# A half step for the value matmuls in an attention scheduler, and its rules in a table by stretch

## The chip, the cores and the metric

The kernel runs on one core of one Trainium2 chip. The metric is device time in microseconds (us), the median of several runs. One further execution was recorded by the hardware profiler, and all views of the profile are of that one. Engines: PE does matmuls (PEld is its weight load), ACT evaluates functions such as exp, DVE and POOL do elementwise work, SP issues most DMAs.

## The reference

Four layers follow each other, each added to a residual stream `x` of 2048 tokens by 512 features, each with 32 heads of 16 features and with a layer norm ahead:

```python
x = x + A(ln(x)); x = x + B(ln(x)); x = x + A(ln(x)); x = x + B(ln(x))

def A(x):                       # full softmax attention
    q, k, v = heads(x @ wqkv)
    p = softmax(einsum("bhqd,bhkd->bhqk", q, k) * Dh ** -0.5)
    return merge(einsum("bhqk,bhkd->bhqd", p, v)) @ wo

def B(x):                       # linear attention with a learned feature map
    q, k, v = heads(x @ wqkv)
    phi = lambda t: concat(softmax(t @ w_phi), softmax(-(t @ w_phi)))
    kv, z = einsum("bhsf,bhsd->bhfd", phi(k), v), phi(k).sum(over s)
    return merge(phi(q) @ kv / (phi(q) . z + 1e-6)) @ wo
```

Both A layers share their weights, and so do both B layers. The change is in A alone.

## The kernel before

`LayerA.attention` emits one A layer, `self.li` being 0 for the first and 1 for the second. The heads are taken in 8 sets of four (`g`), the queries in 4 blocks of 512 (`j`); a pair of these is a group `G`, 32 in all. A group goes over 16 tiles of 128 keys (`kt`). For each key tile there are two *halves* in the sense of heads (`h` is 0 or 1), so a layer has 32 × 16 × 2 = 1024 score tiles of 128 by 1024.

The work of one score tile: `score_cols` (line 1266) issues eight small matmuls side by side on PE, with 32 keys and 512 queries each, into a pair of PSUM banks (`psS`, two such pairs). ACT then takes exp of the whole tile (line 1273) into one of six SBUF buffers `p`. When both tiles of a key tile are there, `pvs` (line 1316) multiplies them with the values: eight fp32 matmuls with 64 keys by 32 value columns as weights and 512 queries as the moving side, summed over the 16 key tiles in a pair of accumulator banks. There are two such pairs, `double` and `pm`; one holds the running group, the other is for everything else.

Some score tiles don't go to ACT. `power_task` lets DVE compute the exponential, with some sixteen instructions per tile (lines 1284 to 1304), into the one buffer `px`. Its scores go into a free pair of accumulator banks, are issued eight key tiles ahead (`LEAD`), and only for groups 1 to 25 (`POWERS`). In the text such a tile is a tile of powers.

Beside these, PE has side work, in two streams of Python generators: the projections of the next octet of heads (`octet`: values, then from a given step on keys and queries, then norms, whose maximum at line 1028 ends the octet), the output projection of finished blocks, and in the first layer the preparation of weights. Side work takes the free pair of banks (`take`) and goes in units of eight matmuls. After the norms come, an event of the scheduler emits the key and query loads of the next two sets of heads (`load_rows` and `load_shift`, lines 1245 to 1253) on SP's queue; the value loads (line 988) are on the same queue.

The order of all this is written out by hand: a planner in Python runs a model of the engines while it emits the instructions. `pe` is the model's time on PE, `act` that on ACT. A score tile counts `UNIT` (0.217 us), a value step `STEP` (0.864), an exp `EXP` (0.904). In each turn of the loop a score tile goes first, as soon as its bank pair is free (`free`). Otherwise the planner asks what fits before the next score tile must start if ACT is not to wait (`due`): first a value step if one is ready, then a tile of powers, then a unit of side work. A value step may end up to `LATE` = 0.2 us after that time. A tile of powers may be issued while side work is pending only from step `EAGER[self.li]` on, 100 in the first attention layer and 0 in the second; `self.now` is the step, that is 16 G + kt, so a layer has 512.

Of the kernel before, what the change touches and what calls it, by code (L numbers as in the profile page):

```python
# [24 lines left out]
NT = S // P  # L25
# [25 lines left out]
FAR = 1e9  # L51
UNIT = 0.217
STEP = 0.864
EXP = 0.904
THERE = 0.54
BACK = 1.11
# [5 lines left out]
POWERS = 26  # L62
LEAD = 8
RING = 4
EAGER = (100, 0)
VBUSY = 0.4
LATE = 0.2
SIDE = 0.0
ALIGN = 0.05
BACKGROUND = 100  # L70
# [7 lines left out]
def mha_hedgehog_stack(ctx, tc, x_in, a_wqkv, a_wo, b_wqkv, b_wphi, b_wo, out, shmin=SHMIN):  # L78
    nc = tc.nc
# [798 lines left out]
    class LayerA:  # L878
# [426 lines left out]
            self.pt[(G, kt, half)] = pt  # L1305
            self.done[(G, kt, half)] = self.plan.end + 0.15

        def pvs(self, G, kt, acc):
            g, j = self.groups[G]
            o, par = g // 2, g % 2  # L1310
            for hh in range(4):
                pt = self.pt[(G, kt, hh // 2)]
                x = kt * 132 + hh * 33 + 17 * par
                for h in range(2):
                    r = slice(64 * h, 64 * h + 64)
                    nc.tensor.matmul(acc[h][32 * hh:32 * hh + 32, :], self.oct[o]["v"][r, x:x + 32],  # L1316
                                     pt[r, hh % 2, :], start=(kt == 0), stop=(kt == NT - 1), skip_group_check=True)

        def load_ob(self, j):
            if j == 0:  # L1320
# [126 lines left out]
        def attention(self, extra, nxt):  # L1447
# [8 lines left out]
            plan = self.plan  # L1456
# [20 lines left out]
            tiles = deque((G, kt, h) for G in range(len(self.groups)) for kt in range(NT) for h in range(2))  # L1477
            pvq = deque((G, kt) for G in range(len(self.groups)) for kt in range(NT))
            estart, slots, acc, pvdone = [], [0.0] * 6, {}, 0
            pe = act = 0.0  # L1480
            self.yts, self.sp = [0.0] * RING, 15.0
            power, pxfree = set(), 0.0
            lost = 0.0
            with tc.manual_schedule(engines=COMPUTE):
                while pvq or any(s.gens for s in self.streams):
                    plan.now = pe
                    plan.advance(pe)
                    for e in list(events):
                        if self.now >= e[0] and e[1]():
                            events.remove(e)  # L1490
                            e[2]()
                    if tiles:
                        free = estart[-2] + BACK if len(estart) > 1 else 0.0
                        due = act - THERE
                        if not slots:
                            free = due = FAR
                        if free <= pe:
                            G, kt, h = tiles.popleft()
                            if (G, kt, h) in power:
                                continue  # L1500
                            self.now = kt + NT * G
                            assert self.groups[G][0] in self.kq
                            self.scores(G, kt, h)
                            slots.sort()
                            start = max(act, pe + THERE, slots.pop(0))
                            lost += start - act
                            act = start + EXP
                            estart.append(start)
                            self.done[(G, kt, h)] = start + BACK
                            pe += UNIT  # L1510
                            continue
                    else:
                        free = due = FAR
                    need = self.side_need()
                    ready = 0
                    for G, kt in pvq:
                        if any(self.done.get((G, kt, h), FAR) > pe for h in range(2)):
                            break
                        ready += 1
                    first = need is not None and need[1][0] == "pe" and len(need[1]) > 2 and ready <= 1  # L1520
                    for turn in range(2):
                        if first == (turn == 0):
                            if need is not None:
                                s, (kind, *what) = need
                                if kind == "M":
                                    soon = pvq and (NT - pvq[0][1] <= ALIGN * what[0] or pvq[0][0] not in acc)
                                    if min(self.pfree) <= pe and not soon:
                                        s.need, s.holds = None, True
                                        break
                                elif pe + what[0] <= (free + SIDE if len(what) == 1 else max(due, free)):  # L1530
                                    plan.now = pe + what[0]
                                    s.need = None
                                    pe += what[0]
                                    self.stream_need(s)
                                    break
                        elif ready:
                            G, kt = pvq[0]
                            if (G in acc or min(self.pfree) <= pe) and pe + STEP <= max(due, free) + LATE:
                                if G not in acc:
                                    acc[G] = self.take()  # L1540
                                pvq.popleft()
                                idx, banks2 = acc[G]
                                self.pvs(G, kt, banks2)
                                if kt == NT - 1:
                                    pvdone = G + 1
                                    self.spawn(self.norm_task(G, idx, banks2), STEP + 0.3)
                                pe += STEP
                                plan.now = pe
                                for h in range(2):
                                    if (G, kt, h) in power:  # L1550
                                        pxfree = pe + 0.3
                                    else:
                                        slots.append(pe + 0.35)
                                    del self.pt[(G, kt, h)]
                                break
                        if turn == 0 and tiles and pxfree <= pe and (need is None or self.now >= EAGER[self.li]) and plan.clock["V"] <= pe + VBUSY:
                            n = NT * tiles[0][0] + tiles[0][1] + LEAD
                            G, kt = n // NT, n % NT
                            if 0 < G < POWERS and self.groups[G][0] in self.kq and plan.now >= self.landed[self.groups[G][0]] and pvq[0][0] in acc and \
                               NT - pvq[0][1] >= 3 and min(self.pfree) <= pe and pe + UNIT <= max(due, free):  # L1560
                                power.add((G, kt, 1))
                                pxfree = FAR
                                idx, ps = self.take()
                                self.score_cols(*self.groups[G], kt, 1, ps)
                                pe += UNIT
                                plan.now = pe
                                self.spawn(self.power_task(G, kt, 1, idx, ps))
                                break
                    else:
                        pe = min(max(free, pe), pe + 0.02) if free > pe else pe + 0.02  # L1570
                        assert pe < 2000.0
                plan.now = FAR / 2
                plan.advance(FAR)
# [707 lines left out]
```

## Time and profile before

| | us |
|---|---|
| runs | 2494.02, 2494.33, 2494.68, median 2494.33 |
| the profiled execution | 2493.94 |
| its span, first to last instruction | 2492.2 |
| first attention layer, first to last exp (71.0 to 1009.2) | 938.2 |
| second attention layer (1311.7 to 2239.7) | 928.0 |
| ACT busy in exp, first and second attention layer | 929.62 (1004 exps), 923.06 (997 exps) |
| mean granted clock of PE | 0.989 |

A row of the matmul order or of the chain begins with the start in us and the length in us. A row of a busy-time view begins with a stretch, from and to, then its length, then busy time and, in parentheses, the number of instructions; behind these stand the granted clock, the share of the DMA engines' time and GB/s. Of the 2048 score tiles of both layers 2001 go to ACT, so 47 are tiles of powers.

### The profile page before, as it was taken

To read this page: it belongs to the slowest core of one execution; us is meant where nothing else is said; L and a number is where in the kernel's file an instruction comes from. 1 tells how busy PE (TensorE), PEld (TensorE's weight loads), DVE (VectorE), ACT (ScalarE), POOL (GpSimd) and SP (SyncE) were. 2 spreads that over 40 slices of the span, in tenths; PEclk is the share of its full clock that TensorE was granted. 3 is DMA by queue.
4 is the path that set the end of the run, shared out by engine and by line. 5 is a ranking of instruction groups with operands and counts; after the bars stand their busy time and mean duration, and the time that the engine had idled before them with its cause. 6 is when DMAs were issued, how large, how long until landed. Compare 5 with 4: busy or idle time off the path is not lost.

```text
span 2492.2 us, 103433 instructions
## 1 busy us (share of the span) xinstructions
PE 2303.5 (92%) x46698; PEld 1083.9 (43%) x46698; DVE 1602.2 (64%) x2866; ACT 2136.6 (86%) x2379; POOL 530.6 (21%) x644
## 2 busy tenths in 40 slices
PE   6999999999989999899889999999999999998998
PEld 4444444444434443445344444444443444444543
DVE  8233456756667455889973666667567652469897
ACT  6899999999999999444539999999999999993553
POOL 3111111121110000356441112111111000005553
PEclk9999999999999999999899999999999999999999
DMA  5412240132045331100124004203300441120003
GB/s 195 69 27 44 49 82 20 43 48 50 3 104 126 118 112 62 52 35 18 61 72 77 19 7 63 34 3 51 65 4 15 88 128 48 66 70 26 26 1 112
DMA packets 114925, 142.86 MB, mean 57 GB/s; under 512 B 64184, under 2 KB 69928, under 8 KB 112168
## 3 DMA queue, kind: packets, MB, share of 16 engines
q1 hardware_dynamic: 113288, 133.38, 21.7%
q8 instruction: 367, 6.01, 1.0%
q0 software_dynamic: 1184, 2.77, 0.3%
q14 instruction: 86, 0.70, 0.1%
HBM read 62.16 MB, written 41.94 MB: 42 GB/s over the span
## 4 chain that ended last, share of the span: by engine, by line
ACT 58%; PE 14%; issue 12%; DVE 12%; POOL 2%; DMA 0%; ACTq 0%; POOLq 0%; SPq 0%; DVEq 0%
ACT p L1273 57%; PE double L1316 3%; PE s L1266 2%; DVE su L1691 1%; PE pbv L1618 1%; PE pk L1618 1%; PE pq L1618 1%; PE pm L713 1%; DVE yt L1908 1%; DVE f L1683 1%; POOL f L1700 1%; DVE f L1684 1%; PE fl L1950 1%; DVE mx L1680 1%; PE pm L1316 1%
## 5 line engine op out<-in xcount | busy, mean ns | idle before, releaser
L1273 ACT ACTIVATE p<-s 128x1024 f32<-128x1024 f32 x2001 | 1853.0, 1063 | 19.2 <-PE s L1266 15.2
L1266 PE MATMUL s<-kq 49*32 49x512 f16 x15136 | 789.7, 381 | 102.7 <-ACT p L1273 86.8
L1266 PEld LDWEIGHTS <-kq 49*32 49x32 f16 x15872 | 385.8, 89 | 881.8 <-issue 795.9
L1316 PE MATMUL double<-p,v 64*32 64x512 f32 x9064 | 612.7, 591 | 0.0
L1316 PE MATMUL pm<-p,v 64*32 64x512 f32 x6944 | 475.6, 589 | 0.0
L977 POOL TENSOR_TENSOR yt<-yt,yt 128x512 f32<-128x512 f32 x64 | 84.8, 1324 | 764.1 <-DVE yt L974 742.3
L1316 PEld LDWEIGHTS double<-p,v 64*32 64x32 f32 x9064 | 174.1, 106 | 30.9 <-issue 6.2
L1618 PEld LDWEIGHTS <-xnTa 128*128 128x128 f16 x1152 | 111.1, 99 | 155.1 <-DVE f L1684 26.4
L1350 DVE SCALAR_TENSOR_TENSOR xt<-pm,c_oA,xt 128x512 f32<-128x512 f32 x102 | 76.2, 747 | 155.9 <-PE pm L713 151.9
L1097 POOL TENSOR_TENSOR sq<-stg 128x512 bf16<-128x512 f16 x48 | 57.7, 1202 | 478.1 <-DVE stg L1005 250.6
L1316 PEld LDWEIGHTS pm<-p,v 64*32 64x32 f32 x6944 | 135.0, 106 | 21.6 <-issue 2.6
L1700 POOL TENSOR_TENSOR f<-f,su 128x1024 f32<-128x1024 f32 x58 | 112.2, 1934 | 116.3 <-DVE su L1694 103.4
L974 DVE STREAM_TRANSPOSE yt<-double 128x512 f32<-128x512 f32 x72 | 47.3, 695 | 112.3 <-PE double L1316 112.1
L1618 PE MATMUL pbv<-wbv,xnTa 128*128 128x512 f16 x384 | 93.9, 397 | 21.7 <-DVE f L1684 21.7
L1685 ACT ACTIVATE f<-f,c_pB 128x1024 f32<-128x1024 f32 x62 | 70.4, 1148 | 49.6 <-DVE f L1684 42.3
L1706 ACT ACTIVATE fk<-f 128x1024 f16<-128x1024 f32 x30 | 31.7, 1057 | 74.7 <-POOL f L1700 74.7
L713 PEld LDWEIGHTS <-wA 64*32 64x32 f16 x4608 | 75.9, 93 | 44.8 <-issue 9.2
L974 DVE STREAM_TRANSPOSE yt<-pm 128x512 f32<-128x512 f32 x56 | 36.8, 696 | 90.4 <-PE pm L1316 90.1
L1000 DVE TENSOR_SCALAR tq<-double,c_qk 128x512 f32<-128x512 f32 x28 | 21.0, 749 | 108.0 <-PE double L713 101.0
L1618 PE MATMUL pq<-wbqk,xnTa 128*128 128x512 f16 x384 | 88.4, 379 | 0.7 <-DVE vt L1645 0.7
L1618 PE MATMUL pk<-wbqk,xnTa 128*128 128x512 f16 x384 | 88.1, 379 | 0.0
L1950 PE MATMUL fl<-wbo,obB 128*128 128x512 f16 x312 | 76.7, 403 | 8.7 <-ACT raw L1902 3.6
(342 smaller groups left out, 3083.2 us busy)
## 6 DMA issues: line engine op xcount, KB each, us to landing
kq<-stg SPq DMA_DIRECT2D x168, 128.0 KB
xd<-xt SPq DMA_DIRECT2D x40, 512.0 KB
xt<-xd SPq DMA_DIRECT2D x40, 512.0 KB
v<-vyt SPq DMA_DIRECT2D x384, 16.0 KB
oD<-osp SPq DMA_DIRECT2D x24, 256.0 KB
ob<-oD SPq DMA_DIRECT2D x8, 768.0 KB
xt<-in_A_x_dram SPq DMA_DIRECT2D x8, 512.0 KB
wbqk<-dBqk SPq DMA_DIRECT2D x2, 2048.0 KB
```

The costliest lines, as they stand in the source:

```text
L713: nc.tensor.matmul(ps[h][c, :], w[r, c], x[r], start=(n == 0), stop=(n == of - 1), skip_group_check=True)
L974: nc.vector.transpose(ys[u].rearrange("p a b -> p (a b)"), ps[u])
L977: nc.gpsimd.tensor_tensor(ys[0], ys[0], ys[1], ALU.add)
L1097: nc.gpsimd.tensor_tensor(sq, hi, hi, ALU.mult)
L1266: nc.tensor.matmul(banks2[u][32 * c:32 * c + 32, :], self.side(g, half, 64 * u, 0, kt * P + 32 * c, 32), self.side(g, half, 64 * u, 1, j * ...
L1273: nc.scalar.activation(pt, s, AF.Exp, scale=EXPS)
L1316: nc.tensor.matmul(acc[h][32 * hh:32 * hh + 32, :], self.oct[o]["v"][r, x:x + 32], pt[r, hh % 2, :], start=(kt == 0), stop=(kt == NT - 1), ...
L1350: nc.vector.scalar_tensor_tensor(xt[:, u, :], ps[h], con["oA"], xt[:, u, :], op0=ALU.mult, op1=ALU.add)
L1618: nc.tensor.matmul(dst, xnT[:, a, c, t * P:(t + 1) * P], w(b, c), start=(i == 0 and c == 0), stop=(i == 2 and c == NC4 - 1))
L1685: nc.scalar.activation(f, f, AF.Exp, scale=con["pB"])
L1700: nc.gpsimd.tensor_tensor(f3, f3, self.part_sums(f3, slice(0, 64), factor), ALU.mult)
L1950: nc.tensor.matmul(ps2[:, u, :], obs[j][:, c, a, t * P:(t + 1) * P], wo[:, b, c, :], start=(c == 0 and i == 0), stop=(c == NC4 - 1 and i = ...
```

## The change

A value step can be parted. `pvs` takes a slice of the 512 queries; a parted step issues its eight matmuls once for queries 0 to 255 and, in a later turn, once more for queries 256 to 511. The model counts `HALF` = 0.434 us for each. Between the two, score tiles and side work may be issued, but no other value step. The first half goes out only where the whole doesn't fit, and never for key tile 0 of a group.

The two constants `LATE` and `EAGER` give way to a table `RULES` with a row per attention layer and an entry per stretch of 32 steps. An entry has three numbers. The first says when a tile of powers may be issued: 2 always, 1 only with no side work pending, 0 never. The second is the lateness allowed to a whole step or a second half, the third that allowed to a first half. The first layer has entries of its own for each stretch; the second has (2, 0.02, 0.0) throughout.

```diff
+HALF = 0.434
-EAGER = (100, 0)
-LATE = 0.2
+RULES = (((2, 0.2, 0.05), (2, 0.2, 0.05), (2, 0.05, 0.01), (2, 0.1, 0.01), (2, 0.02, 0.2), (2, 0.02, 0.1), (2, 0.05, 0.0), (2, 0.02, 0.1),
+          (2, 0.05, 0.1), (2, 0.2, 0.0), (2, 0.02, 0.05), (2, 0.1, 0.1), (2, 0.02, 0.2), (0, 0.02, 0.02), (2, 0.02, 0.01), (1, 0.02, 0.02)),
+         ((2, 0.02, 0.0),) * 16)
...
-        def pvs(self, G, kt, acc):
+        def pvs(self, G, kt, acc, part=slice(0, 512)):
...
-                    nc.tensor.matmul(acc[h][32 * hh:32 * hh + 32, :], self.oct[o]["v"][r, x:x + 32],
-                                     pt[r, hh % 2, :], start=(kt == 0), stop=(kt == NT - 1), skip_group_check=True)
+                    nc.tensor.matmul(acc[h][32 * hh:32 * hh + 32, part], self.oct[o]["v"][r, x:x + 32],
+                                     pt[r, hh % 2, part], start=(kt == 0), stop=(kt == NT - 1), skip_group_check=True)
...
+                    eager = RULES[self.li][self.now // 32][0]
...
-                            if (G in acc or min(self.pfree) <= pe) and pe + STEP <= max(due, free) + LATE:
+                            room = max(due, free) - pe
+                            late, short = RULES[self.li][self.now // 32][1:]
+                            if half is not None and HALF <= room + late:
+                                pvq.popleft()
+                                idx, banks2 = acc[G]
+                                self.pvs(G, kt, banks2, slice(256, 512))
+                                half, step = None, HALF
+                            elif half is None and (G in acc or min(self.pfree) <= pe) and (STEP <= room + late or kt and HALF <= room + short):
                                 if G not in acc:
                                     acc[G] = self.take()
+                                idx, banks2 = acc[G]
+                                if STEP > room + late:
+                                    self.pvs(G, kt, banks2, slice(0, 256))
+                                    half = kt
+                                    pe += HALF
+                                    plan.now = pe
+                                    break
                                 pvq.popleft()
-                                idx, banks2 = acc[G]
                                 self.pvs(G, kt, banks2)
+                                step = STEP
+                            else:
+                                step = None
+                            if step:
...
-                        if turn == 0 and tiles and pxfree <= pe and (need is None or self.now >= EAGER[self.li]) and plan.clock["V"] <= pe + VBUSY:
+                        if turn == 0 and tiles and pxfree <= pe and (eager == 2 or eager and need is None) and plan.clock["V"] <= pe + VBUSY:
```

More of the change, by code (lines that the diff above doesn't have):

```diff
@@ L1481, in attention @@
             self.yts, self.sp = [0.0] * RING, 15.0
-            power, pxfree = set(), 0.0
+            power, pxfree, half = set(), 0.0, None
             lost = 0.0
@@ L1537, in attention @@
                             G, kt = pvq[0]
-                            if (G in acc or min(self.pfree) <= pe) and pe + STEP <= max(due, free) + LATE:
+                            room = max(due, free) - pe
[6 more added lines that the diff above has]
+                            elif half is None and (G in acc or min(self.pfree) <= pe) and (STEP <= room + late or kt and HALF <= room + short):
                                 if G not in acc:
                                     acc[G] = self.take()
+                                idx, banks2 = acc[G]
[5 more added lines that the diff above has]
+                                    break
                                 pvq.popleft()
-                                idx, banks2 = acc[G]
                                 self.pvs(G, kt, banks2)
+                                step = STEP
+                            else:
+                                step = None
+                            if step:
                                 if kt == NT - 1:
                                     pvdone = G + 1
-                                    self.spawn(self.norm_task(G, idx, banks2), STEP + 0.3)
-                                pe += STEP
+                                    self.spawn(self.norm_task(G, idx, banks2), step + 0.3)
+                                pe += step
                                 plan.now = pe
```

## The prediction

> **What bounds the kernel now.** I read the page first, then busy time by stage, then the chain of waits in two stretches of 40 us, then the order of the matmuls around one irregular place of that chain.
>
> ```profile
> PE 2303.5 (92%) x46698; PEld 1083.9 (43%) x46698; DVE 1602.2 (64%) x2866; ACT 2136.6 (86%) x2379; POOL 530.6 (21%) x644
> ACT 58%; PE 14%; issue 12%; DVE 12%; POOL 2%; DMA 0%; ACTq 0%; POOLq 0%; SPq 0%; DVEq 0%
> L1273 ACT ACTIVATE p<-s 128x1024 f32<-128x1024 f32 x2001 | 1853.0, 1063 | 19.2 <-PE s L1266 15.2
> ```
> ```profile
> 71.00:543.20 472.20, 466.36 (x503) 1.00 0.24 45
> 71.00:1009.20 938.20, 929.62 (x1004) 1.00 0.27 64
> 1311.70:2239.70 928.00, 923.06 (x997) 1.00 0.23 49
> ```
> The second fence is ACT's busy time in exp (line 1273) by stretch: from, to, length, busy, count. The two attention stages last 938.2 and 928.0 us, 1866 of the span's 2492, and ACT is busy in 99% of both. PE's 92% on the page looks like a rival bound, but the chain runs 58% over ACT. So each attention stage takes as many exps as it holds, times the interval from one exp to the next, and the change can act through these two numbers alone.
>
> The interval is where the time hides. ACT's records (1063 ns) are longer than the interval and overlap, so an exp may start late without any idle time: the 15.2 us of waiting for scores says little. The starts in the chain of waits say more:
>
> ```profile
> 603.24 0.71 ACT p L1273
> 603.94 0.20 issue
> 604.14 0.88 ACT p L1273
> 605.02 0.04 issue
> 605.07 1.63 ACT p L1273 x2
> 606.69 0.37 issue
> 607.07 0.70 ACT p L1273
> ...
> 622.58 1.63 ACT p L1273 x2
> ...
> 633.68 1.63 ACT p L1273 x2
> ```
> ```profile
> 1607.85 1.63 ACT p L1273 x2
> ...
> 1625.36 1.63 ACT p L1273 x2
> ...
> 1636.46 1.63 ACT p L1273 x2
> ```
> From 603.24 to 604.14 is 0.90, the shortest interval; two exps take 1.83 (603.24 to 605.07). The two merged into "x2" take 2.00 (605.07 to 607.07): 0.17 too much. What PE did there:
>
> ```profile
> 604.53 0.41 PE L1266 MATMUL s<-kq 49*32 49x512 f16 x8
> 604.75 1.05 PE L1316 MATMUL pm<-p,v 64*32 64x512 f32 x16
> 605.61 0.41 PE L1266 MATMUL s<-kq 49*32 49x512 f16 x8
> 605.82 0.41 PE L1266 MATMUL double<-kq 49*32 49x512 f16 x8
> 606.20 0.41 PE L1266 MATMUL s<-kq 49*32 49x512 f16 x8
> 606.41 1.05 PE L1316 MATMUL pm<-p,v 64*32 64x512 f32 x16
> 607.27 0.41 PE L1266 MATMUL s<-kq 49*32 49x512 f16 x8
> ```
> A score tile holds PE for 0.22 (604.53 to 604.75), a value step for 0.86 (604.75 to 605.61), together 1.08 against the 0.90 that ACT needs for one exp. The score buffers forgive one such step in two exps. When a second step follows behind the next score (here one had preceded 604.53), the score after it is 0.17 late, and ACT with it. The planner lets that happen: LATE is 0.2, and 0.17 is less.
>
> **The change part by part.** *(1) Tighter lateness, with halves as the way out.* In the second attention stage a whole step may now end only 0.02 late, a half not at all; in the first stage the table keeps 0.2 for wholes in stretches 0, 1 and 9 and gives 0.1 to 0.02 elsewhere. After a whole step has used up the slack, the room behind the next score is 0.90 − 0.22 = 0.68: a whole (0.86) is refused, a half (0.43) fits and leaves 0.25. So the 0.17 should go. How often does it occur? Three "x2" in each of the two stretches of 40 us above, 0.075 per us; over 938 and 928 us that is 70 and 70, an estimate, worth 12.0 and 11.8 us. Three of the first stage's 16 stretches keep their rule, which leaves 13/16 × 12.0 = 9.7, together 21.5. I take three quarters, 16: some halves of the first stage may still be late by up to 0.2, and a queue of value steps that drains more slowly can stall something else. Bounds: 0 and 21.5; beside that, halves in the place of wholes can save the 0.01 or 0.02 that a single whole step costs (I count nothing, at most 6 over both stages).
>
> *(2) What a split costs PE.* A whole step has 16 matmul records and 16 weight loads, a split one 32 and 32. No half step is in the trace. The nearest rows: 16 matmuls of 512 fp16 columns, two units of side work, on the same 64x32 tiles, and the 16 loads of a whole value step:
>
> ```profile
> 1319.06 0.61 PE L713 MATMUL pm<-xnTb,wAv 64*32 64x512 f16 x16
> 1319.49 0.40 PE L1266 MATMUL s<-kq 49*32 49x512 f16 x8
> ```
> ```profile
> 604.53 0.36 PEld L1316 LDWEIGHTS pm<-p,v 64*32 64x32 f32 x16
> ```
> Sixteen pairs of load and matmul pass in 0.43 (1319.06 to 1319.49), which is half of 0.86. And 16 fp32 loads take 0.36, less than 0.43, so they can lie under the matmuls. I cost the split at nothing; what covers a small excess is the 0.25 left behind a half. The other bound: if no load were hidden, a half would take 0.43 + 0.36, that is 0.36 too long, 0.11 more than the cover; 13/16 × 70 + 70 = 127 split steps have 254 halves, 28 us. A gain is excluded, since the columns are the same. I take 0, because the fp16 row has the same count of loads and matmuls on the same tiles.
>
> The Trainium skill speaks against this: its page "TensorEngine Tiling (Array Packing)", section "Instruction Overhead", gives each matmul some 60 cycles of overhead on this chip and warns against splitting a small dimension. At the 2.4 GHz of "TensorE: Matmul & The Clock Gate" (its opening table) that would be 25 ns, an estimate, 0.4 us for the 16 extra matmuls one behind another, and 127 × (0.4 − 0.25) = 19 us of loss by it. The row at 1319.06 doesn't show it: its matmuls follow each other at 27 ns each over eight tiles, with no room for an overhead on top.
>
> *(3) Tiles that DVE computes.* Each tile of powers takes an exp from ACT. Before, the first stage allowed one with side work pending only from step 100 on; now from the start. DVE's first instruction of that task, two per tile:
>
> ```profile
> 71.00:255.00 184.00, 0.00 (x0) 0.99 0.26 41
> 1311.70:1495.00 183.30, 6.78 (x10) 0.98 0.18 35
> ```
> None in the first 184 us of stage one; ten, so five tiles, in the first 183 us of stage two, which already worked by the new rule. I add five. Each saves an exp (0.90), but its scores (605.82 is one such place) crowd an exp interval and may cost 0.17 where the table still allows it: 5 × (0.90 − 0.17) = 3.7 us. Bounds: 0 (no pair of banks free, because the weight preparation runs there too) and 8 × 0.90 = 7.2. DVE's own time is hidden, since ACT bounds the stage.
>
> *(4) What these tiles push back.* A tile of powers holds one of the two pairs of accumulator banks, which the projections of the next octet need.
>
> ```profile
> 272.73 0.40 PE L1266 MATMUL pm<-kq 49*32 49x512 f16 x8
> ```
> ```profile
> 275.24 0.69 DVE L1287 SCALAR_TENSOR_TENSOR pw<-px,pm 128x512 f32<-128x512 f32 x1
> ```
> ```profile
> 243.07 0.16 DVE L1028 TENSOR_REDUCE nmx<-nm 128x1 f32<-128x4 f32 x1
> ```
> ```profile
> 1505.00 0.15 DVE L1028 TENSOR_REDUCE nmx<-nm 128x1 f32<-128x4 f32 x1
> ```
> The pair is held from 272.73 to 275.93, 3.2 us, five times 16. The octet's end (line 1028) comes 172 us into the first stage (243.07 − 71.0) and 193 us into the second (1505.00 − 1311.7), which has the five tiles: 21 us later. By the new rule I expect the first stage's octet 1 some 16 to 21 us late. Its own keys don't mind, but octet 2 queues behind it, and its last DMAs, the shift rows, have this room:
>
> ```profile
> 525.34 5.03 SPq L1253 DMA_DIRECT2D kq<-sh x8
> ```
> ```profile
> 71.00:543.20 472.20, 12.28 (x18) 1.00 0.24 45
> ```
> They are issued by 530.4. Group 16, which reads them, starts after 256 × 2 tiles; nine of those before it are powers (line 1284, the second row, 18 instructions), so after 503 exps, which the second fence has at 543.2: 12.8 us of room. The earlier gains pull this need forward by the five tiles (3.7) and by the doubled steps of stretches 2 to 7 (353 us × 0.075 × 0.17 = 4.5), to 535. A slip of 21 carried whole to the rows (551) would make PE, and ACT with it, wait 16 us. But octet 2 has slack of its own; eight key and query columns (line 1000) take longer in the first stage than in the second:
>
> ```profile
> 313.00:497.10 184.10, 5.96 (x8) 1.00 0.22 48
> 1551.00:1706.70 155.70, 6.00 (x8) 1.00 0.18 27
> ```
> If it runs like the second (155.7 instead of 184.1) the 28 us swallow the slip. Between 0 and 16 I take 4, nearer to nothing, because octet 2 begins only at step 132 in either kernel and so part of the slip ends there. Queues: no DMA is added or moved past another by hand; the key loads of line 1245 to 1253 share SP's queue with the value loads as before.
>
> **Sum.** The profiled execution took 2493.94 us, 1.7 more than its span; the median of the runs is 2494.33, 0.4 away, so one scale serves both. 2493.94 − 16 (doubled steps) − 0 (splits) − 3.7 (powers) + 4 (late keys) = 2478.2, forecast 2478. The linear attention layers are not touched.
>
> **The rivals.**
>
> *The wait moves to the p buffers (0.14).* Six p buffers hold three steps; a step is worked off in two halves instead of at once, so the buffers may come free one interval late, and ACT waits for them what it waited for scores. For it: PE is busy in 92% of the span. Against it: no row above has ACT waiting for a value step. Term 1 falls to 0, price 2493.94 − 3.7 + 4 = 2494.
>
> *The keys of group 16 come late (0.08), the other side.* If octet 2 takes no slack back and its values, too, wait for pairs held by powers, the slip grows beyond the 21 seen. The wait is the slip less the room that is left, 535 − 530.4 = 4.6. It eats the gain of 16 + 3.7 = 19.7 at a slip of 24, and from 29 on the kernel is measurably slower. At 36, which is the 21 and as much again as the five tiles hold the pair (16, and rounded down), the wait is 31: 2478 − 4 + 31 = 2505. Against it: the second stage shows 21, not 36.
>
> *A half costs PE more than half (0.05), also slower.* At the full 0.11 over the cover, 2478 + 28 = 2506; it takes back the whole gain from 16/254 = 0.06 per half over the cover.
>
> *All of it comes (0.13).* 21.5 instead of 16, eight powers, no late keys: 2493.94 − 21.5 − 7.2 = 2465.
>
> **How the numbers follow.** My forecast has 0.60, with its own range of 2468 to 2488 (term 1 from 8 to 21.5, term 4 from 0 to 8). A measurement of this kernel can tell 0.2%, 5 us, from no change. Faster: 0.60 + 0.13 and 0.02 of the first rival, 0.75. The same: the 0.12 left of that rival. Slower: 0.08 + 0.05 = 0.13. The range goes from 2465, where all of it comes, over the no-change rival at 2494 to 2497; the two slower cases and a little of the best are left out.
>
> **What would show it.** Right on (1): in the chain, "x2" of exps followed by 0.37 become rare in the second stage, its length falls by 8 to 12 us at about 997 exps; in the order of PE, matmuls of 256 columns stand behind scores. Right on (2): from the first matmul of a half to the next score is 0.43 to 0.44. Right on (3): about ten instructions of line 1284 in the first 184 us of stage one, and about 999 exps there. (4): PE waits for key DMAs near 535, or doesn't. The forecast is wrong if ACT starts to wait for p buffers, if a half takes over 0.5, if the first stage shows a gap of 10 us or more before group 16, or if the count of powers falls: each one lost costs 0.90.

## The result and the profile after

The changed kernel takes 2501.92 us (median of 7 runs, 2498.50 to 2505.12), the kernel before on the same chip 2494.33 (7 runs, 2491.84 to 2496.61): a ratio of 1.003, with an interval from 1.0018 to 1.0042. It is slower by 0.3%; I had forecast 2478. The profiled execution, the shortest of the seven, took 2498.50 us with a span of 2496.7.

By stage, the changed kernel's busy times; the columns are from, to, length, then busy time and count of PE, its weight loads, DVE, ACT and POOL, and the granted clock, the DMA share and GB/s:

```profile
70.70:1005.60 934.90, 887.11 (x22505) 427.47 (x22506) 542.86 (x973) 922.17 (x1001) 112.39 (x107) 1.00 0.26 62
1005.70:1323.20 317.50, 272.39 (x2019) 139.48 (x2019) 283.10 (x488) 134.75 (x178) 156.58 (x254) 0.96 0.15 47
1323.20:2245.40 922.20, 878.97 (x22516) 418.18 (x22515) 526.45 (x930) 917.72 (x999) 110.72 (x103) 1.00 0.22 50
2245.40:2496.70 251.30, 223.24 (x1587) 107.87 (x1584) 220.08 (x349) 108.77 (x142) 125.32 (x125) 0.97 0.12 43
```
The same second stretch of the kernel before, from the end of the first attention layer's exps to the start of the second's:

```profile
1009.20:1311.70 302.50, 268.99 (x1973) 137.25 (x1957) 269.43 (x459) 134.87 (x178) 157.05 (x254) 0.97 0.14 44
```
Both attention layers became shorter, 934.9 after 938.2 and 922.2 after 928.0. What was lost lies between them, in the linear attention layer, whose code the change doesn't touch: 317.5 us after 302.5. DVE is busy there for 89% of the time in both kernels, and it has 13.7 us more to do (283.10 after 269.43), 29 instructions more. PE is as busy as DVE there before (89%) and less so after (86%); its work grew by 3.4 us only (272.39 after 268.99). The sum −3.3 + 15.0 − 5.8 − 1.2 (behind the second layer, before 252.5) with −0.3 at the start is 4.4 of the spans' 4.5.

What DVE does there that it didn't do before: the output adds of query block 2 (line 1352 now, 1350 before). First the adds within that stretch, in the changed kernel and in the one before, then the places of the last of them in the changed kernel, whose exps end at 1005.6:

```profile
1005.70:1323.20 317.50, 2.91 (x4) 0.96 0.15 47
```
```profile
1009.20:1311.70 302.50, 0.00 (x0) 0.97 0.14 44
```
```profile
1008.27 0.71 DVE L1352 SCALAR_TENSOR_TENSOR xt<-pm,c_oA,xt 128x512 f32<-128x512 f32 x1
...
1010.71 0.71 DVE L1352 SCALAR_TENSOR_TENSOR xt<-double,c_oA,xt 128x512 f32<-128x512 f32 x1
```
The adds are 2.9 us themselves. The norm's statistics and the transposes of the same tokens follow them and fall behind the last exp too. Before, the last of these transposes came behind it as well, but sooner. Here is where they start (line 1386 before, 1388 now) and, from the chain of waits, a multiplication of the linear layer on POOL, the eleventh of its line in both; first the kernel before, then the changed one:

```profile
1019.57 0.66 PE L1386 MATMUL double<-ident,xn 128*128 128x128 f32 x4 [0.30 <-DVE xn L575]
...
1084.65 1.94 POOL f L1700
```
```profile
1033.35 1.97 PE double L1388 x8
...
1094.80 1.94 POOL f L1720
```
Counted from the end of the exps, the transposes start after 10.4 us before and after 27.8 now, and POOL's multiplication after 75.5 and 89.2: 13.7 of the 15.0 us are lost by then. From 1007.67 to 1033.31 the chain of the changed kernel runs over DVE almost without a break. During attention all this lies under ACT's exps; behind it there is no cover.

The two things that I had said to look for at the start of the first layer are both there. The tiles of powers (line 1286, two instructions each) in its first 184 us, and the end of octet 1:

```profile
70.70:255.00 184.30, 6.83 (x10) 0.99 0.17 29
```
```profile
274.31 0.15 DVE L1030 TENSOR_REDUCE nmx<-nm 128x1 f32<-128x4 f32 x1
```
Five tiles, as forecast; octet 1 ends at 274.31 instead of 243.07, 31 us late where I expected 16 to 21. The half steps, in the order of matmuls of the second layer:

```profile
1606.10 0.41 PE L1268 MATMUL s<-kq 49*32 49x512 f16 x8
1606.32 0.40 PE L1318 MATMUL pm<-p,v 64*32 64x256 f32 x4
1606.34 0.39 PE L1318 MATMUL pm<-px,v 64*32 64x256 f32 x4
1606.53 0.40 PE L1318 MATMUL pm<-p,v 64*32 64x256 f32 x4
1606.56 0.38 PE L1318 MATMUL pm<-px,v 64*32 64x256 f32 x4
1606.86 0.41 PE L1268 MATMUL s<-kq 49*32 49x512 f16 x8
1607.07 0.40 PE L1318 MATMUL pm<-p,v 64*32 64x256 f32 x4
...
1607.51 0.41 PE L715 MATMUL double<-xnTb,wA 64*32 64x512 f16 x8
```
Here a key tile with a tile of powers is worked off in halves around a score tile. From the second half's first matmul to the side work behind it is 0.44 (1607.07 to 1607.51). From the first half's to the score behind it is 0.54 (1606.32 to 1606.86); a score can have to wait until ACT has emptied its bank pair (95 such waits of PE in the second layer, 34.2 us), so this is no measure of the half itself. In the chain of waits from 1600 to 1640 no exps are merged into an "x2" any more.

### The profile page after: what moved, and what is told of

It reads as the page before. It is cut to its first block, busy times and chain, and to the rows that moved or that the text cites. A ratio compares the mean times of both kernels' runs of the same rounds, so it can differ in the third digit from the quotient of the medians.

```text
span 2496.7 us, 107999 instructions
## 1 busy us (share of the span) xinstructions
PE 2309.6 (93%) x48986; PEld 1125.4 (45%) x48986; DVE 1630.0 (65%) x2882; ACT 2123.7 (85%) x2378; POOL 530.2 (21%) x644
## 4 chain that ended last, share of the span: by engine, by line
ACT 58%; DVE 14%; PE 13%; issue 12%; POOL 2%; DMA 0%; POOLq 0%; ACTq 0%; SPq 0%; DVEq 0%
ACT p L1275 57%; PE s L1268 2%; PE pm L1318 2%; DVE su L1711 2%; PE pk L1638 1%; DVE yt L1928 1%; PE double L1318 1%; PE pbv L1638 1%; PE pq L1638 1%; POOL f L1720 1%; DVE f L1703 1%; DVE yn L1938 1%; DVE f L1704 1%; DVE mx L1700 1%; DVE su L1712 1%
## 5 line engine op out<-in xcount | busy, mean ns | idle before, releaser
L1318 PE MATMUL pm<-p,v 64*32 64x512 f32 (+1 forms) x12152 | 748.4, 540 | 0.6 <-issue 0.5
L1318 PE MATMUL double<-p,v 64*32 64x512 f32 (+1 forms) x5864 | 366.4, 547 | 0.3 <-issue 0.3
L1318 PEld LDWEIGHTS pm<-p,v 64*32 64x32 f32 x12152 | 238.1, 106 | 36.4 <-issue 4.7
L1352 DVE SCALAR_TENSOR_TENSOR xt<-double,c_oA,xt 128x512 f32<-128x512 f32 x98 | 73.1, 746 | 155.3 <-PE double L715 154.0
L976 DVE STREAM_TRANSPOSE yt<-pm 128x512 f32<-128x512 f32 x86 | 56.5, 695 | 137.0 <-PE pm L1318 137.0
L1318 PEld LDWEIGHTS double<-p,v 64*32 64x32 f32 x5864 | 114.8, 106 | 17.4 <-issue 1.8
L715 PE MATMUL double<-woA,ob 64*32 64x512 f16 x2304 | 93.4, 375 | 2.4 <-issue 2.4
L1970 PE MATMUL fl<-wbo,obB 128*128 128x512 f16 x312 | 75.5, 398 | 9.5 <-ACT raw L1922 4.0
```

What stands on the lines that cost most here:

```text
L715: nc.tensor.matmul(ps[h][c, :], w[r, c], x[r], start=(n == 0), stop=(n == of - 1), skip_group_check=True)
L976: nc.vector.transpose(ys[u].rearrange("p a b -> p (a b)"), ps[u])
L1318: nc.tensor.matmul(acc[h][32 * hh:32 * hh + 32, part], self.oct[o]["v"][r, x:x + 32], pt[r, hh % 2, part], start=(kt == 0), stop=(kt == NT ...
L1352: nc.vector.scalar_tensor_tensor(xt[:, u, :], ps[h], con["oA"], xt[:, u, :], op0=ALU.mult, op1=ALU.add)
L1970: nc.tensor.matmul(ps2[:, u, :], obs[j][:, c, a, t * P:(t + 1) * P], wo[:, b, c, :], start=(c == 0 and i == 0), stop=(c == NC4 - 1 and i = ...
```

## The experiments

The theory after this result, S: the early powers push the side work back, its tail is left over at the end of the first attention layer, and DVE pays for it in the linear layer. Its first rival, H: the halves and the tight lateness push the side work back. The second: the long stretch has another cause. All kernels are the changed one with the edit shown; ratios are to the kernel before, on the chip of that comparison.

**The first layer by the old rules, the second by the new.**

```diff
-eager = RULES[self.li][self.now // 32][0]
+eager = RULES[1][0][0] if self.li or self.now >= 100 else 1
-late, short = RULES[self.li][self.now // 32][1:]
+late, short = RULES[self.li][self.now // 32][1:] if self.li else (0.2, -FAR)
```


> The first attention layer keeps the old rules (lateness 0.2, no halves, powers with side work pending from step 100), the second has the new ones. Both theories on the lost time (S: the early powers push the side work back and leave the tail of query block 2 to DVE in the linear layer; H: halves and the tight lateness push it back) expect the stretch between the two attention layers back at 302 to 304 us from 318, the first layer at 937, the second at 921, so 2494 - 6 = 2488. If the 15 us of that stretch come from neither (a third possibility: from something that the second layer's new order moves), the stretch stays at 318 and the time near 2502.

Ratio 0.9991 (0.9981 to 1.0001), no clear difference. The stretch between the layers, in its trace:

```profile
1011.00:1313.30 302.30, 267.54 (x1980) 137.18 (x1965) 269.14 (x459) 134.59 (x178) 156.59 (x254) 0.97 0.14 44
```
It is back, so the loss comes from the first layer's rules. The second layer's rules were to give 6 us; between the medians it is 2 (2494.56 beside 2496.57), not clear of nothing.

**The first layer by the new rules, the second by the old.**

```diff
-late, short = RULES[self.li][self.now // 32][1:]
+late, short = (0.2, -FAR) if self.li else RULES[self.li][self.now // 32][1:]
```


> The first attention layer has the new rules, the second the old ones. S and H expect the first layer at 934 and the stretch behind it at 318 as in the changed kernel, the second layer back at 927: 6 more than the changed kernel, about 2508. If the new rules of the second layer are worth nothing, it stays at 2502.

Ratio 1.0032 (1.0018 to 1.0047), 2503.57 us beside 2496.57: the same loss as the whole change. I had expected 6 us more than that, so here, too, the second layer's rules show no worth. The stretch is 317.8 us.

**The new table, but powers from step 100 on as before.**

```diff
-eager = RULES[self.li][self.now // 32][0]
+eager = RULES[1][0][0] if self.li or self.now >= 100 else 1
```


> The changed kernel, but in the first layer powers may be issued with side work pending only from step 100 on, as before; halves and lateness by the new table. S: octet 1 ends near 243 again instead of 274, the stretch between the layers returns to about 304, the first layer takes 934 to 938, time 2486 to 2490. H: the side work is late all the same, the stretch stays at 312 to 318, time 2498 to 2503.

Ratio 0.9945 (0.9932 to 0.9959), 2483.48 us beside 2496.57: faster than the kernel before and, by the ratios, than the changed one. Octet 1 ends at 248.4, the last output add of query block 2 starts 9 us before its last exp, and the stretch is

```profile
1006.70:1308.00 301.30, 268.06 (x1955) 136.53 (x1953) 267.08 (x444) 135.00 (x178) 156.57 (x254) 0.97 0.13 43
```
Taking away nothing but the early powers turned the loss into a gain, as S had it. (The edit also overrides the table's first numbers for stretches 13 and 15, but these never act: tiles of powers are issued eight key tiles ahead and for groups up to 25 only, so none is left after step 407.)

**Only the early powers; value steps whole and late by up to 0.2 in both layers.**

```diff
-late, short = RULES[self.li][self.now // 32][1:]
+late, short = 0.2, -FAR
```


> Of the change only the earlier powers of the first layer are left; value steps are whole, lateness 0.2 in both layers. S: octet 1 ends near 270, the stretch between the layers is 312 to 318, so the kernel is slower than before by 5 to 12 us, 2499 to 2506. H: the side work is as before, the stretch is 304, and the six more tiles of powers save 4 us: 2490.

Ratio 1.0028 (1.0018 to 1.0039), 2505.04 us. Octet 1 ends at 278.7. The stretch, and the first layer's exps:

```profile
1017.60:1329.60 312.00, 273.23 (x1980) 139.52 (x1963) 277.75 (x468) 134.71 (x178) 156.70 (x254) 0.95 0.14 46
```
```profile
70.90:1017.60 946.70, 925.03 (x997) 0.99 0.26 62
```
The early powers alone make the kernel slower, by 8.5 us between the medians. The profiled execution is the longest of the eight, 2511.95 us, so its two stretches together show about twice that. Seven exps fewer than before, and yet the layer takes 946.7 us there: the starts of the exps lose some 6.5 us in five gaps between 537 and 548, where group 16 begins. The waits of PE from 530 to 550 in that kernel (total in us, count, longest) name the keys' DMA:

```profile
PE s L1268 <- DMA kq<-sh: 2.6, 4, 0.8
```
That is the wait for late keys that my prediction had priced, 2.6 us of the 6.5 as PE sees it, the rest not accounted for; in the changed kernel there is no such gap at that place. As much again is lost in longer gaps elsewhere in the layer (23.3 us in gaps above 0.2 us, 8.8 before), in this one execution.

**Octet 1 held back, without early powers.** Old rules in both layers; the one edit beside them:

```diff
+if self.li == 0 and o == 1:
+    yield "n", 16
 self.start_octet(o, self.next_w, False)
```


> The old rules in both layers, and one thing else: in the first attention layer octet 1's projections begin only at step 16, some 29 us later. No early powers, no halves. S (late side work alone costs the time): octet 1 ends near 270, output adds of query block 2 are left for after the last exp, the stretch between the layers grows from 303 to 310 or more, and the kernel is slower than before by 5 to 15 us. Rival (the early powers cost by themselves, through DVE or the order in the linear layer): the stretch stays at 303 and the time within 3 us of before.

Ratio 1.0001 (0.999 to 1.0012): S was wrong here. Octet 1 ends at 279.9, later than in the changed kernel, but octets 2 and 3 take it back (500.5 and 695.6, before 492.4 and 677.0, changed 513.2 and 713.6), the last output add comes 8 us before the last exp, and the stretch is 301.1 us. The 8 us are not all slack won back: in this execution (2499.56 us, the median is 2497.56) the exps themselves end later, the layer taking 945.0 us, and the last add starts at 1007.4, 0.9 us later than before. So a late octet 1 is not enough. What counts is where the chain of side work stands when the exps end.

**No halves, lateness 0.02 everywhere, old powers.**

```diff
-eager = RULES[self.li][self.now // 32][0]
+eager = RULES[1][0][0] if self.li or self.now >= 100 else 1
-late, short = RULES[self.li][self.now // 32][1:]
+late, short = 0.02, -FAR
```


> Old powers, lateness 0.02 in both layers, no halves at all. If the halves are what makes the tight rule affordable, the value steps queue here, ACT waits elsewhere or side work is late, and the time is 4 us or more above the next kernel (tight with halves). If tightness alone does it, doubled steps vanish in the same way and both are within 3 us, near 2484.

Ratio 1.0111 (1.0096 to 1.0126), 2525.63 us. The waits of ACT for scores over the whole kernel, and a piece of its matmul order in the second layer:

```profile
ACT p L1275 <- PE s L1268: 45.2, 62, 5.0
```
```profile
1390.65 0.41 PE L1268 MATMUL s<-kq 49*32 49x512 f16 x8
1390.86 1.27 PE L715 MATMUL pm<-xnTb,wA 64*32 64x512 f16 x40
1391.94 1.05 PE L1318 MATMUL double<-p,v 64*32 64x512 f32 x16
1392.80 0.63 PE L1268 MATMUL s<-kq 49*32 49x512 f16 x16
```
The wait of 15.2 us before is 45.2 here. Where a whole step is refused behind a score, five units of side work go instead (40 matmuls from 1390.86 on), then the whole step, and the next score comes 2.15 us after the last (1390.65 to 1392.80). In the planner's code a score tile waits while none of the six `p` buffers is free, and only value steps free them; that this held the score back here is read from the code, not from the trace. Without halves, the tight rule costs 16 us more than with them (the next kernel).

**Halves, lateness 0.02 and 0 in both layers, no table; old powers.**

```diff
-late, short = RULES[self.li][self.now // 32][1:]
+late, short = 0.02, 0.0
```


> Old powers, the second layer's rule (0.02 for wholes, 0 for halves) in both layers, no table by stretch. Since the second layer lost nothing by it and the table's loose entries keep 14 doubled steps, I expect the same as with the table or 1 to 3 us better: 2481 to 2485, against 2496 for the kernel before on that chip. If the table by stretch matters, 2488 or more.

Ratio 1.0049 (1.0035 to 1.0063), 2509.81 us: my expectation was wrong. The first layer's exps are as short as with the table (933 us), but the stretch behind is the longest of all:

```profile
1005.10:1327.70 322.60, 274.30 (x2020) 139.79 (x2016) 283.57 (x488) 134.99 (x178) 157.05 (x254) 0.94 0.14 46
```
Octet 1 is on time (246.4), octet 3 ends at 717.8, and four output adds fall behind the last exp. H holds too, then: the tight rule alone, with the old powers, can push the side work past the end. The table's looser entries are what keeps it inside.

**Halves, but lateness 0.2 for wholes; old powers.**

```diff
-late, short = RULES[self.li][self.now // 32][1:]
+late, short = 0.2, 0.0
```


> Old powers, lateness 0.2 as before, halves allowed where a whole step doesn't fit even so. If the gain is the lateness rule, the doubled steps stay (60 to 70 in each layer) and the time is that of the kernel before within 4 us. If halves help by themselves, by starting value work earlier, it is 2490 or less.

Ratio 1.0 (0.9989 to 1.001). By the starts of the exps, 70 and 61 of them are late by 0.14 to 0.2 us, as before (67 and 65). But hardly any halves were issued: this trace has 64 matmuls of 256 columns, two parted steps, where the changed kernel has 4576, which is 143 steps. Where wholes may be late by 0.2, a whole nearly always fits first. So the gain doesn't come with the loose rule; what halves would do by themselves, this kernel can't say.

**Only the tail held back.** Old rules in both layers, and

```diff
 ln = Norm([], f"a{self.li}_{j}")
+if self.li == 0 and j == 2:
+    yield "n", 508
 for t2 in range(2):
```


> The old rules in both layers; the one difference is that in the first attention layer the tail of query block 2 (its last output adds, norm and transposes) is held back until step 508 of 512. No halves, no early powers, no other octet moved. S in its new form (it is the tail left over at the last exp that costs, because DVE bounds the linear layer): output adds fall behind the last exp, the stretch between the layers grows from 303 to 315 or more with 10 us or more of DVE work added to it, and the kernel is 8 to 20 us slower than before. Rival (the leftover only goes along with the long stretch and something else makes it long): the stretch stays at 303 to 306, the time within 4 us of before.

Ratio 1.0064 (1.0051 to 1.0078), 2512.43 us beside 2495.87. The stretch, and the last add, 7 us behind the last exp (1013.4):

```profile
1014.30:1333.00 318.70, 274.62 (x2012) 139.65 (x2004) 283.33 (x490) 134.71 (x178) 157.27 (x254) 0.95 0.15 46
```
```profile
1020.80 0.75 DVE L1352 SCALAR_TENSOR_TENSOR xt<-pm,c_oA,xt 128x512 f32<-128x512 f32 x1
```
Without early powers, halves or another order of the octets, a tail left over makes the same stretch as in the changed kernel: 318.7 us with 283.3 of DVE, beside 317.5 with 283.1. This shows the cause of the 15 us directly.

**The changed kernel without the first layer's late powers.**

```diff
-eager = RULES[self.li][self.now // 32][0]
+eager = RULES[self.li][self.now // 32][0] if self.li or self.now < 256 else 0
```


> The changed kernel, early powers and all, but in the first layer no powers are issued from step 256 on, so that the side work has the free pair of banks to itself there. If the powers' hold on that pair is what makes the side work late, it catches up: first output add before 740 instead of 746, none after the last exp, the stretch between the layers 302 to 305. Some eight powers fewer cost 7 us of exps, so 2502 - 15 + 7 = 2494, near the kernel before. If it is the tight lateness and the halves, the output adds stay late, the stretch stays at 312 or more, and the time is above 2502.

Ratio 1.0011 (1.0 to 1.0022). Octet 1 is as late as in the changed kernel (275.9), but without powers from step 256 on the chain catches up: octet 3 ends at 694.5, the first output add starts at 725.4 instead of 746.3, none falls behind the last exp, and

```profile
1016.70:1315.60 298.90, 265.13 (x1956) 135.58 (x1949) 264.52 (x440) 134.78 (x178) 156.60 (x254) 0.98 0.14 42
```
So in the changed kernel the late chain pays for the powers behind step 256. Whether by their hold on the pair or by DVE's time, which they take as well, this run doesn't separate. Ten tiles fewer (1011 exps instead of 1001) take the gain away again.

**The first layer's table alone, with the old powers.** The kernel with powers from step 100 on, and the second layer by the old rules:

```diff
-late, short = RULES[self.li][self.now // 32][1:]
+late, short = (0.2, -FAR) if self.li else RULES[self.li][self.now // 32][1:]
```


> The kernel with the old start of the powers and the new table (e3), but the second attention layer has the old rules: what is the first layer's table worth alone? In the profiles the first layer took 933 instead of 937 and the stretch behind it 302 instead of 303, so by these -5.4 of 2496: a ratio of 0.998. By the times (e3 0.9945, second layer alone 0.9991) it would be 0.9954.

Ratio 0.9967 (0.9955 to 0.9979), 2489.88 us, between my two estimates.

**The kernel with powers from step 100 on once more,** beside the one above:

> The same kernel as e3 once more, beside the run above on one chip, so that the second layer's rule is the difference of the two. By the profiles' mean of the second layer (old 927.6, new 924.2) the difference is 3 us; by my prediction's term for that layer 9 to 12. Ratio to before 0.993 to 0.997.

Ratio 0.9964 (0.995 to 0.9978), 2487.73 us. It beats the kernel before a second time. The second layer's rule is worth 2 us between these two medians, within what the intervals leave open; the second layer's exps took 925.3 us by the old rules here and 920.0 by the new:

```profile
1311.00:2236.30 925.30, 921.41 (x997) 1.00 0.23 50
```
```profile
1310.20:2230.20 920.00, 916.98 (x999) 1.00 0.23 50
```
Over all profiles, from first to last exp, the second layer took 924.4 to 929.0 us by the old rules (seven of them, one with loose halves allowed) and 919.1 to 924.6 by the new with the changed kernel's table (five); the kernel with tight halves and no table, with the same numbers there, took 930.5. The single profile scatters by as much as the effect.

## Why the prediction was wrong

**(1) The doubled steps: right in mechanism, smaller in sum.** I had 140 of them, worth 23.8 us, from two stretches of 40 us with three each; that six events came so close is partly luck. Counted by the starts of all exps against an interval of 0.904 us, 132 lay 0.14 to 0.2 us late before, 22.9 us together, and 21 in the changed kernel, 3.6 us. So 19.2 went, more than the 16 of my term. But exps late by 0.005 to 0.03 rose from 1096 to 1434, from 14.8 to 20.3 us, which I had priced at nothing or a gain, and gaps above 0.2 us in the first layer from 8.8 to 15.7. With three powers more in the first layer and two fewer in the second, what is left is the 3.3 + 5.8 = 9.1 us by which the two stages shrank, where terms (1) and (3) together had 19.7. Without the early powers, the rest of the change gave 13 and 9 us between the medians.

**(2) The split at nothing: right.** 143 steps were parted, where I had 127. 16 matmuls of 256 columns pass in 0.43 to 0.44 where side work stands behind them. My sign, 0.43 to 0.44 to the next score, was badly chosen: the median of 212 such places is 0.54, as a score can wait for ACT. The rule of the Trainium skill that spoke against it, 60 cycles of overhead for each matmul ("TensorEngine Tiling (Array Packing)", section "Instruction Overhead"), doesn't show here: by the trace a split step takes what a whole one does, 2 × 0.43 against 0.86.

**(3) Five early powers: right in count, wrong in worth.** The first 184 us hold five. Over the layer it is three, since the first layer's count rose from 20 to 23 only: the exps went from 1004 to 1001. I had a gain of 3.7 us; alone they cost 8.5, through what they push back.

**(4) The step that failed.** "What these tiles push back" saw the slip, 16 to 21 us forecast and 31 measured at octet 1 (some 5 of them are there without early powers), and followed it to the nearest wait, the keys of group 16, where I put 4 us. There nothing was lost in the changed kernel. I stopped following, and so the linear layer stood in the sum at nothing, where it cost 15.0 us. Behind octet 2 come octet 3 (677.0, now 713.6), the output projections (first add 727.2, now 746.3) and the tail of block 2, whose last add came 2 us before the last exp and now comes 6 us after it. The sentence "The linear attention layers are not touched" was true of their code and wrong of their time. I had the rows for it: DVE's 269.43 us of 302.50 in that stretch, on the view by stage that I used for ACT alone, would have shown that work left over there has no cover. Each gain in the exps also pulls the end forward by its own size, so the shorter attention and the later side work ran towards each other. Between the forecast (15.7 us less) and the profiled execution (4.6 more) lie 20 us: 15.0 in the linear layer, 10.6 that terms (1) and (3) fell short, less the 4 for keys that were not late and 1.5 elsewhere.

How the place of the last output add stands to the stretch behind, for seven of the kernels:

| kernel | last add after last exp, us | stretch, us | ratio |
|---|---|---|---|
| powers from step 100 (e3) | −9.1 | 302.3 | 0.9945 |
| octet 1 held back | −7.6 | 302.0 | 1.0001 |
| before | −1.8 | 303.4 | 1 |
| only early powers | 3.5 | 313.0 | 1.0028 |
| changed | 6.0 | 318.5 | 1.003 |
| tight halves, no table | 5.9 | 323.6 | 1.0049 |
| tail held back | 7.4 | 319.7 | 1.0064 |

(From last to first exp start, thus one exp longer than the rows above.) Each stretch is of one profiled execution. For the three at 313.0, 323.6 and 319.7 that one is the longest of its kernel's runs, 3 to 7 us above the median; for the changed kernel it is the shortest, 3.4 below. So a few microseconds mean nothing here. Ahead of the last exp the place costs little: six further traces with the last add there, 0.9 to 14.5 us ahead, have stretches of 299.9 to 306.6. From there on it costs more than the delay itself, 10 to 20 us for 3.5 to 7.4.

**The rivals.** The late keys, my case on the slower side, happened in the kernel with the early powers alone, with some 6.5 us around it and not 31. The move of the wait to the `p` buffers is seen in no trace as such: ACT's waits before exps are for scores in every kernel (15.2 us before, 21.0 in the changed one, 45.2 without halves). Without halves the planner, by its code, holds the scores back for them. A half cost no more than half a step. The case that came was none of mine.

**What stays open.** Why the one rule for all stretches makes octet 3 end at 717.8 and the table at 705.7, with 19 and 18 tiles of powers, was not shown. That value halves go ahead of side units in the planner's turns, and a shorter layer leaves PE less room for them, is only argued. Whether the powers delay the side work by the pair of banks or by DVE's time was not separated, nor whether the 15 us are DVE's added work or the chain of waits through it. Nor do the single profiles say in which gaps the first layer's table alone gains its 0.3%.

## What to carry to other kernels

Work that is hidden under a bound engine has a deadline, the end of that engine's work, and whoever delays it must follow it to there and not to the next wait alone; look at which engine bounds the stage behind, since the leftover is paid at that engine's price. When a change shortens a stage and delays its side work at once, add the two before comparing with the slack. And a change with two parts is worth trying one at a time: here the new table without the early powers gained 0.4 to 0.55%, and the early powers on top of it took 0.7 to 0.85% (1.003 beside 0.9964 and 0.9945).

## What the runs showed that I had not expected

- A leftover of four output adds (2.9 us), with its norm and transposes, lengthens the linear layer by 15 us, about as much as DVE's added busy time there (13.7 us).
- Octet 1 may be 37 us late (279.9 instead of 243.1) at no measurable cost (1.0001), because the chain behind it has slack of its own: octet 3 is only 19 us late (695.6 after 677.0), and the last add less than 1 us (1007.4 after 1006.5).
- Tight lateness without halves costs 1.1%, and under loose lateness the planner hardly issues a half (two steps): neither part of that rule works alone.
